# A decode block of attention and a ReLU layer: a weight piece split 126 to 2, a product in four column groups, and one head's softmax moved ahead of a loop

## The chip, the cores and the metric

The kernel runs on one core of a Trainium2 chip. The metric is device time in microseconds (us), lower is better. Before the change three runs gave 355.25, 355.38 and 355.55; the median is 355.38.

The core has five instruction streams that run side by side and wait for each other through semaphores: PE (TensorE, matrix products; its weight loads are listed as PEld), DVE (VectorE), ACT (ScalarE), POOL (GpSimd) and SP (SyncE, which here issues nearly all DMAs). Sixteen DMA engines move data between HBM and the on-chip memory SBUF. Matrix products land in PSUM.

## The reference

One token passes through a block whose layer norms are modulated by a condition `c`: grouped attention over a cache of 32768 positions (32 query heads, 8 key and value heads of 128), an output product, then a ReLU layer 512 to 1792 to 512.

```python
mod = (_silu(c) @ w_mod).reshape(c.shape[0], 6, 1, -1)     # sa, ca, ga, sb, cb, gb
h = _layernorm(x) * (1 + ca) + sa
q = (h @ wq) as 32 heads of 128
scores = q . k_cache / sqrt(128);  p = softmax(scores);  o = p . v_cache     # 4 query heads share one k, v
x = x + ga * (o @ wo)
h = _layernorm(x) * (1 + cb) + sb
x = x + gb * (relu(h @ w1) @ w2)
```

All inputs are bfloat16. The caches are 2 x 64 MB; with the weights 149 MB are read, and each byte is used once.

## The kernel before

**Data.** All bulk loads are issued by SP in one fixed order, the list `stream` (L139 to L144): w_mod, wq, K of head 0 in two pieces of 4 MB, then for each head the pieces of the next head's K and this head's V in turn, the last head's V in three pieces, wo in four pieces (WOP, L47: heads 0 to 3, 4 and 5, 6, 7), w1 in two, w2 in six (W2P, L51: 4, 3, 3, 2, 1 and 1 of 14 row blocks, 1 KB a row and block). `need(key)` (L147) issues the stream up to the piece that is asked for; `load` (L96) makes the destination. The destinations are five slots of a ring (L74), so an issue waits until the slot's last reader is done. An issue also waits for the eighth issue before it, because eight DMA semaphores take turns.

**A head.** K arrives as rows. `turn_k` (L405) transposes a quarter of a head's K on DVE in place (128x2048 words), `scores` (L422) multiplies each quarter with the queries (32 matmuls for half a head), and `bank_max` (L428) copies the half's scores to SBUF and takes maxima. `softmax` (L432 to L475) is a generator; each `next` does one step of it: m_p on DVE; the transpose mT on PE; Mrow and Mexp on DVE; the transpose Mb on PE, nbias and the exponentials P_g on ACT; their transpose PT_g and the sums Lexp on DVE; L_ps on PE; Linv on DVE. `pv` (L477) multiplies probabilities with V, 64 columns of steps in 32 matmuls for half a head. For heads 0 to 5, and the first half of head 6, these 32 stand in a hardware loop inside a section (L490 to L496) that is scheduled as one block; elsewhere they are written out. `blocks`, `o_cols` and `normalise` (L509 to L540) bring a head's output into a column and divide by the sums; `spread` (L544) and `project` (L555) multiply with wo.

**Order.** PE and DVE run in the order in which the program is written (L599). The main loop (L611) handles head g's V together with head g+1's K. In its second half it transposes and scores the second half of the next head's K, calls `bank_max`, starts the next head's softmax with one `next` (m_p), runs `pv(g, (2, 3))`, and does one more `next` (mT). The rest of that softmax is spread over the first half of the following round, between the four K quarters there (L618, L622, L631, L637, L640). With g = 6 the loop goes on differently (L653 to L664), then follow head 7's V, the wo product and the layer.

**The end.** Small filler products (`keep_clock`, L592) stand between the dependent steps. The attention output is brought into columns, `layernorm_T` (L250) makes the second layer norm, meanwhile `four_rows` (L331) turns the residual into four rows of 128 with a product whose weights are `rowpick`, 128x4. w1's product goes to four rows of PSUM at partitions 0, 32, 64 and 96 (L714), is transposed on DVE (L724), and ReLU on ACT (L725) writes it into `hid_bd`, which holds for each row block and each quarter i of the output a 128x4 matrix that is zero but for column i. The last product (L735) is 14 x 4 matmuls, each with such weights of four columns and 128 columns of w2, all adding into one 4x128 tile, `ffn_ps`. Two DVE products (L740, L742) apply gb and the residual, and SP stores four rows of 128.

Of the kernel before, what the change touches and what calls it, by code (L numbers as in the profile page):

```python
# [9 lines left out]
BF16 = mybir.dt.bfloat16  # L10
F32 = mybir.dt.float32
ACT = mybir.ActivationFunctionType
# [5 lines left out]
def kernel(  # L18
# [31 lines left out]
    LOOPED = Hkv - 2  # L50
    W2P = [(0, 4), (4, 7), (7, 10), (10, 12), (12, 13), (13, 14)]  # L51
    W1P = [(0, KT - 1), (KT - 1, KT)]
    assert Dh == 128 and REP == 4 and D == 512 and FT == W2P[-1][1] and NTILE == 4
    scale = float(Dh) ** -0.5
    eps = 1e-5
# [5 lines left out]
    vv = A_v_cache[0].rearrange("g (p j) d -> g p j d", p=P)  # L61
    wm_v = w_mod.rearrange("(p kt) n -> p kt n", p=P)
    wq_v = A_wq.rearrange("(p kt) n -> p kt n", p=P)
    def wo_v(i):
        g0, n = WOP[i]
        return A_wo[g0 * REP * Dh:(g0 + n) * REP * Dh, :].rearrange("(p r) d -> p r d", p=P)

    w1_v = B_w1.rearrange("(p kt) f -> p kt f", p=P)
    w2_v = B_w2.rearrange("(p f) d -> p f d", p=P)

# [19 lines left out]
    def piece(name, at, n):  # L90

        if name not in pieces:
            pieces[name] = ring.tile([P, 2 * TK * Dh], BF16, tag="slot", name=name)
        return pieces[name][:, at:at + n]

    def load(key):  # L96
        kind = key[0]
        if kind == "wm":
            t = ring.tile([P, KT, 6 * D], BF16, tag="slot", name="wm_sb")
            src = wm_v  # L100
        elif kind == "wq":
            t = ring.tile([P, KT, Hq * Dh], BF16, tag="slot", name="wq_sb")
            src = wq_v
        elif kind in "kv":
            g, steps = key[1], key[2]
            src = (kv if kind == "k" else vv)[g, :, TK * steps[0]:TK * (steps[-1] + 1), :]
            name = "Ksb" if kind == "k" else "Vsb"
            if len(steps) == 2:
                t = ring.tile([P, TK * len(steps), Dh], BF16, tag="slot", name=name)
            else:  # L110
                t = piece(name, TK * Dh * (steps[0] % 2), TK * Dh).rearrange("p (j d) -> p j d", d=Dh)
        elif kind == "wo":
            g0, n = WOP[key[1]]
            t = piece("wo_sb", g0 * REP * D, n * REP * D).rearrange("p (r d) -> p r d", d=D)
            src = wo_v(key[1])
        elif kind == "w1":
            k0, k1 = W1P[key[1]]
            t = piece("w12_sb", k0 * Dff, (k1 - k0) * Dff).rearrange("p (kt f) -> p kt f", f=Dff)
            src = w1_v[:, k0:k1]
        else:  # L120
            f0, f1 = W2P[key[1]]
            t = piece("w12_sb", KT * Dff + f0 * D, (f1 - f0) * D).rearrange("p (f d) -> p f d", d=D)
            src = w2_v[:, f0:f1]
        stream_dma(t[:], src)
        if kind in "kv":
            for i, u in enumerate(steps):
                loaded[(kind, g, u)] = t[:, TK * i:TK * (i + 1), :]
        else:
            loaded[key] = t[:]

    def stream_dma(dst, src):
        i = nc.sync.dma_start(out=dst, in_=src)
        tc.stamp_issue_order_token(i.ins, "sp_stream")
        if last_loop:

            tc.add_manual_dep(i.ins, last_loop[0], mybir.DependencyInfo(
                mybir.DependencyClass.NoSync, mybir.DependencyReason.DATA))

    stream = [("wm",), ("wq",)] + [("k", 0, (2 * G, 2 * G + 1)) for G in range(NG)]  # L139
    for g in range(LAST):  # L140
        for G in range(NG):
            stream += [(kind, gg, (2 * G, 2 * G + 1)) for kind, gg in (("k", g + 1), ("v", g))]
    stream += [("v", LAST, (0, 1)), ("v", LAST, (2,)), ("v", LAST, (3,))] + [("wo", i) for i in range(len(WOP))]
    stream += [("w1", i) for i in range(len(W1P))] + [("w2", i) for i in range(len(W2P))]  # L144
    pos = [0]

# [37 lines left out]
    for n in sorted({n * REP for _, n in WOP}):  # L184
# [21 lines left out]
    nc.vector.tensor_reduce(  # L206
        out=place32[:], in_=ident_f[:].rearrange("p (j m) -> p m j", m=32), op=ALU.add, axis=AX.X,
    )
    rowpick = const.tile([P, KT], F32)
    nc.vector.tensor_reduce(  # L210
        out=rowpick[:], in_=ident_f[:].rearrange("p (j m) -> p j m", m=32), op=ALU.add, axis=AX.X,
    )
    hid_bd = const.tile([P, FT, KT, KT], BF16)
    nc.gpsimd.memset(hid_bd[:], 0.0)

    pick8 = const.tile([16, 8], BF16)
    nc.vector.tensor_tensor(out=pick8[:], in0=ident_bf[0:16, 0:8], in1=ident_bf[0:16, 8:16], op=ALU.add)
# [22 lines left out]
    def bank(name):  # L240
        return ps_s.tile([P, 512], F32, tag="s", name=name)[:]
# [88 lines left out]

    def four_rows(e, name):  # L331

        r_ps = bank(f"{name}_ps")[0:KT, 0:P]
        nc.tensor.matmul(  # L334
            r_ps, lhsT=rowpick[:], rhs=e[:].rearrange("p m kt -> p (m kt)"), start=True, stop=True,
        )
        return r_ps

    gb_rows = const.tile([KT, P], F32)
    nc.scalar.copy(out=gb_rows[:], in_=four_rows(expand(modT_sb[:, 5 * KT:6 * KT], "gb"), "gb"))  # L340

    hT = const.tile([P, KT], BF16)
# [36 lines left out]
    def build_qbd(g):  # L379
        d_ap = qbd[g % 2][:]  # L380
        d_ps = d_ap.ap[0][0]
        s_ap = qrep_sb[:]
        s_ps = s_ap.ap[0][0]
        for a in range(4):
            o = AP(d_ap.tensor, d_ap.offset + (32 * a) * d_ps + 4 * 7 + 32 * a,
                   [[d_ps, 32], [QW, 4], [1, 4]])
            i = AP(s_ap.tensor, s_ap.offset + (32 * a) * s_ps + REP * g,
                   [[s_ps, 32], [Hq, 4], [1, 4]])
            nc.scalar.copy(out=o, in_=i)  # L389
# [209 lines left out]
    with tc.manual_schedule(engines={mybir.EngineType.PE, mybir.EngineType.DVE}):  # L599
# [10 lines left out]
        soft = None  # L610
        for g in range(LAST):  # L611
            h = g + 1
            build_qbd(h)
            turn_k(h, 0, 0)
            turn_k(h, 0, 1)
            turn_k(h, 1, 0)
            scores(h, 0, 0)
            if soft:  # L618
                next(soft)
            open_o(g)  # L620
            scores(h, 0, 1)
            if soft:  # L622
                next(soft)
            if g > 0:
                blocks(g - 1)
            scores(h, 1, 0)
            if g > 0:
                o_cols(g - 1)
            turn_k(h, 1, 1)
            scores(h, 1, 1)  # L630
            if soft:  # L631
                next(soft)
            if g > 0:
                normalise(g - 1)
                if g in [sum(w) for w in WOP]:
                    spread(part_of(g - 1))
            if soft:  # L637
                next(soft)
            bank_max(h, 0)
            next(soft or iter(()), None)  # L640
            pv(g, (0, 1))
            for u in (2, 3):
                for half in range(2):
                    turn_k(h, u, half)
                    scores(h, u, half)
            bank_max(h, 1)
            soft = softmax(h)
            next(soft)
            if g < LOOPED:
                pv(g, (2, 3))  # L650
                next(soft)
                continue
            next(soft)  # L653
            next(soft)
            pv(g, (2,), range(6))
            next(soft)
            next(soft)
            open_o(LAST)
            pv(g, (2,), range(6, 16))
            pv(g, (3,))  # L660
            next(soft)
            next(soft, None)
            a_rows.append(row_bank("a_ps"))
            blocks(g)  # L664
# [38 lines left out]

        keep_clock(3)
        layernorm_T(x1T[:], stat2, h2T[:], modT_sb[:, 3 * KT:4 * KT], ncb[:], "ln2", meanwhile)
        x1_rows = const.tile([KT, P], F32)
        nc.vector.tensor_copy(out=x1_rows[:], in_=x1_ps[0])

        NQ = 32 * FT
        for part, (k0, k1) in enumerate(W1P):  # L710
# [8 lines left out]
        keep_clock(3)  # L719
        hidT = rows_sb("hidT").rearrange("p a b -> p (a b)")[:, 0:NQ].rearrange("p (f e) -> p f e", e=32)  # L720
        hid_v = hid_ps[:, 0:NQ].rearrange("p (e f) -> p f e", f=FT)
        hb = hid_bd[:]
        for f0, f1 in ((0, FT // 2), (FT // 2, FT)):
            nc.vector.transpose(out=hidT[:, f0:f1], in_=hid_v[:, f0:f1])  # L724
            nc.scalar.activation(  # L725
                out=AP(hb.tensor, hb.offset + KT * KT * f0, [hb.ap[0], [KT * KT, f1 - f0], [KT + 1, KT]]),
                in_=hidT[:, f0:f1, 0:1].to_broadcast([P, f1 - f0, KT]), func=ACT.Relu,
            )

        ffn_ps = bank("ffn_ps")[0:KT, 0:P]  # L730
        for part, (f0, f1) in enumerate(W2P):
            w2_sb = need(("w2", part))
            for ft in range(f0, f1):
                for i in range(KT):
                    nc.tensor.matmul(  # L735
                        ffn_ps, lhsT=hid_bd[:, ft, i, :], rhs=w2_sb[:, ft - f0, i * P:(i + 1) * P],
                        start=(ft == 0 and i == 0), stop=(ft == FT - 1 and i == KT - 1),
                    )
        o_rows = const.tile([KT, P], F32)
        nc.vector.tensor_tensor(out=o_rows[:], in0=ffn_ps, in1=gb_rows[:], op=ALU.mult)  # L740
        o_bf = const.tile([KT, P], BF16)
        nc.vector.tensor_tensor(out=o_bf[:], in0=o_rows[:], in1=x1_rows[:], op=ALU.add)  # L742
    nc.sync.dma_start(out=out[0, 0].rearrange("(i n) -> i n", i=KT), in_=o_bf[:])


# [28 lines left out]
```

## Time and profile before

| | |
|---|---|
| median of three runs | 355.38 us (355.25 to 355.55) |
| the profiled execution: its time, and the span of its records | 355.74 us, 353.9 us |
| PE busy | 279.8 us (79%) |
| DVE busy | 203.1 us (57%) |
| ACT, POOL busy | 25.4 us, 3.9 us |
| HBM read | 149.42 MB, 422 GB/s over the span |
| last product's matmuls (L735) | 347.89 to 351.20 |

The span is the time from the first to the last record of one execution. Times below are counted from its start, so a line "307.78 7.12" is work that began at 307.78 us and took 7.12. A wait is named by what ended it. "Issue to landing" of a DMA is the time from its issue on SP to its last byte's semaphore. The granted clock is the share of TensorE's full clock that the hardware let through.

### The profile page before, as it was taken

What the parts mean: (1) busy time and instruction counts of PE and PEld (TensorE: products, weight loads), DVE (VectorE), ACT (ScalarE), POOL (GpSimd) and SP (SyncE); (2) the same over time, 40 slices, a digit from 0 to 9 for tenths busy, and PEclk for the clock granted to TensorE, in tenths of its full rate; (3) what the DMA queues carried; (4) which work ended last, traced back from release to release, by engine and by line L of the source; (5) the groups of instructions that cost most, each with busy time, mean ns of one, the idle gap of its engine ahead of it and who ended that gap; (6) DMA issues with size and microseconds to landing.
All of it is one profiled execution on the core that took longest, in us unless ns stands there. A gap on an engine that the chain in (4) does not pass through costs nothing. (4 is left out here: it accounts for less than half of the span.)

```text
span 353.9 us, 4006 instructions
## 1 busy us (share of the span) xinstructions
PE 279.8 (79%) x1311; PEld 112.7 (32%) x1311; DVE 203.1 (57%) x271; ACT 25.4 (7%) x69; POOL 3.9 (1%) x16
## 2 busy tenths in 40 slices
PE   0542781999898979897979796979689687989996
PEld 0221230333343323332323232323234233334444
DVE  6245775882768268462939178553938095734142
ACT  1220003000010001000100001000100010002000
POOL 4000000000000000000000000000000000000000
PEclk9995997799899999998999899999999997999999
DMA  8999999999999999999999999999999999999994
GB/s 309 455 422 445 431 422 441 441 418 424 459 418 422 459 418 424 441 437 426 433 444 417 430 456 419 427 446 426 422 448 430 422 439 441 422 430 424 421 420 177
DMA packets 6852, 149.59 MB, mean 423 GB/s; under 512 B 824, under 2 KB 1080, under 8 KB 1976
## 3 DMA queue, kind: packets, MB, share of 16 engines
q1 hardware_dynamic: 6776, 149.43, 98.4%
q8 instruction: 8, 0.13, 0.1%
q14 instruction: 4, 0.03, 0.0%
q0 software_dynamic: 64, 0.00, 0.0%
HBM read 149.42 MB, written 0.00 MB: 422 GB/s over the span
## 5 line engine op out<-in xcount | busy, mean ns | idle before, releaser
L405 DVE STREAM_TRANSPOSE Ksb<-Ksb 128x2048 f32<-128x2048 f32 x64 | 142.9, 2281 | 63.9 <-DMA Ksb<-in_A_k_cache_dram 63.9
L484 PE MATMUL o_ps<-Vsb,PT_g 128*16 (+1 forms) x512 | 130.0, 395 | 21.5 <-ACT qbd L389 7.2
L422 PE MATMUL S_ps<-Ksb,qbd 128*128 128x512 bf16 x512 | 121.8, 388 | 23.5 <-DVE Ksb L405 21.9
L422 PEld LDWEIGHTS <-qbd 128*128 128x128 bf16 x512 | 49.0, 98 | 87.6 <-issue 31.8
L484 PEld LDWEIGHTS o_ps<-Vsb,PT_g 128*16 x416 | 37.4, 90 | 90.2 <-issue 63.7
L428 DVE TENSOR_SCALAR_CACHE_REDUCE S_g<-S_ps 128x512 f32<-128x512 f32 x16 | 11.0, 690 | 34.4 <-PE S_ps L422 34.4
L389 ACT COPY qbd<-qrep_sb 32x16 bf16<-32x16 bf16 x32 | 6.4, 201 | 138.7 <-PE S_ps L422 137.6
L465 DVE STREAM_TRANSPOSE PT_g<-P_g 128x1024 bf16<-128x1024 bf16 x8 | 9.7, 1218 | 6.6 <-ACT P_g L459 6.6
L484 PEld LDWEIGHTS <-PT_g 128*16 128x16 bf16 x96 | 8.2, 90 | 11.0
L456 ACT ACTIVATE nbias<-Mb_ps 128x1 f32<-128x1 f32 x8 | 1.4, 171 | 136.8 <-PE Mb_ps L454 136.8
L459 ACT ACTIVATE P_g<-S_g,nbias 128x1024 bf16<-128x1024 f32 x8 | 9.2, 1148 | 0.2
L227 PE MATMUL xc_ps<-cx_sel,cx_bd 16*128 16x2 bf16 x4 | 0.3, 172 | 11.1 <-DVE cx_bd L221 11.1
L515 DVE SCALAR_TENSOR_TENSOR Y<-o_ps,smask,Y 16x128 f32<-16x128 f32 x24 | 8.1, 339 | 0.8
L471 PE MATMUL L_ps<-Lexp,ones_f 128*128 128x4 f32 x16 | 3.0, 257 | 4.3 <-DVE Lexp L468 4.3
L597 PE MATMUL spare_ps<-qbd,ident_bf 128*128 128x512 bf16 x19 | 5.6, 380 | 0.0
L440 PE MATMUL mT_ps<-ident_f,m_p 128*1 128x128 f32 x8 | 2.2, 270 | 3.9 <-DVE m_p L437 2.0
L471 PEld LDWEIGHTS L_ps<-Lexp,ones_f 128*128 128x128 f32 x16 | 3.1, 221 | 5.8 <-issue 5.1
L443 DVE TENSOR_REDUCE Mrow<-mT_ps 1x4 f32<-1x128 f32 x8 | 2.1, 257 | 4.6 <-PE mT_ps L440 4.6
L534 DVE TENSOR_TENSOR oT_sb<-acc_ps,Linv 128x4 bf16<-128x4 f32 x8 | 1.2, 150 | 5.7 <-PE acc_ps L521 5.7
L295 PE MATMUL mod_ps<-wm_sb,siluT 128*1 128x512 bf16 x24 | 3.6, 624 | 1.0 <-DVE siluT L289 1.0
L505 DVE MEMSET o_ps<- 16x512 f32 x8 | 3.9, 485 | 0.8
L552 DVE CAST o_sb<-o_ps 128x4 bf16<-128x4 f32 (+2 forms) x4 | 0.7, 167 | 5.7 <-PE o_ps L548 5.7
(115 smaller groups left out, 80.0 us busy)
## 6 DMA issues: line engine op xcount, KB each, us to landing
Ksb<-in_A_k_cache_dram SPq DMA_DIRECT2D x16, 4096.0 KB, 35.6
Vsb<-in_A_v_cache_dram SPq DMA_DIRECT2D x15, 4096.0 KB, 35.2
wq_sb<-in_A_wq_dram SPq DMA_DIRECT2D x1, 4096.0 KB, 19.6
Vsb<-in_A_v_cache_dram SPq DMA_DIRECT2D x2, 2048.0 KB, 31.8
wm_sb<-in_w_mod_dram SPq DMA_DIRECT2D x1, 3072.0 KB, 10.4
wo_sb<-in_A_wo_dram SPq DMA_DIRECT2D x1, 2048.0 KB, 29.1
w_sb<-in_B_w_dram SPq DMA_DIRECT2D x1, 1344.0 KB
wo_sb<-in_A_wo_dram SPq DMA_DIRECT2D x1, 1024.0 KB, 31.1
```

Of the source, the lines that this page charges most:

```text
L295: nc.tensor.matmul(dst[j // 4][32 * (j % 4):32 * (j % 4) + 1, :], lhsT=src_T[:, kt:kt + 1], rhs=w[:, kt, j * 512:(j + 1) * 512], start=(kt ...
L389: nc.scalar.copy(out=o, in_=i)
L405: t = nc.vector.transpose(out=KTt.bitcast(F32), in_=KTt.bitcast(F32))
L422: nc.tensor.matmul(S_ps_tiles[g], lhsT=qbd[g % 2][:, hp, 4 * (7 - s):4 * (7 - s) + P], rhs=KTv[:, 16 * sl:16 * sl + 16, h, :, par], start= ...
L428: nc.vector.tensor_scalar(out=S_tiles[g][:, G, :], in0=S_ps_tiles[g], scalar1=1.0, scalar2=None, op0=ALU.mult, op1=ALU.max, accum_out=m_ti ...
L459: nc.scalar.activation(out=P_g[:], in_=S_g[:].rearrange("p g f -> p (g f)"), func=ACT.Exp, bias=nbias[:], scale=scale, accum_out=l_g[:],)
L465: nc.vector.transpose(out=PT_g[:], in_=P_g[:])
L471: nc.tensor.matmul(L_ps[:], lhsT=ones_f[:], rhs=Lexp[:], start=True, stop=True)
L484: nc.tensor.matmul(o_tiles[g][:], lhsT=PT, rhs=Vx, start=False, stop=False, skip_group_check=True)
L505: nc.vector.memset(o_tiles[g][:], 0.0)
L515: nc.vector.scalar_tensor_tensor(out=Y[:], in0=o[:, s], scalar=smask[:, s:s + 1], in1=Y[:], op0=ALU.mult, op1=ALU.add,)
L597: nc.tensor.matmul(spare[0], lhsT=ident_bf[:], rhs=qbd[0][:, :, 0:P], start=True, stop=True)
```

## The change

1. The second piece of w2 (`EVEN`) is loaded by two DMAs, partitions 0 to 125 and 126 to 127, instead of one.
2. wo's last two pieces (heads 6 and 7) are loaded by one DMA instead of two.
3. `rowpick` is 128x128 with the four picking columns at 0, 32, 64 and 96, so that `four_rows` puts its rows on these partitions. gb's rows, the residual's rows and the output rows use all 128 partitions. The store takes every 32nd.
4. The hidden vector is kept plainly, 128x14 (`hid`). Each of the 56 matmuls of the last product has one column of it as weights and writes one row, at partition 32 i for quarter i, so four different column groups of the array are used in turn. `ffn_ps` is zeroed by DVE ahead of w1's product, and all matmuls add to it.
5. In the round g = 5, four more steps of head 6's softmax (mT; Mrow and Mexp; Mb, nbias and P_g; PT_g and Lexp) are written ahead of `pv(5, (2, 3))`; L_ps follows it.
6. In the round g = 6 (`ahead`), the fourth K quarter of the first half is transposed with the first three, Linv follows directly, and all four quarters are scored before `o_cols(5)`.

```diff
@@ -50,6 +50,7 @@
     LOOPED = Hkv - 2
     W2P = [(0, 4), (4, 7), (7, 10), (10, 12), (12, 13), (13, 14)]
     W1P = [(0, KT - 1), (KT - 1, KT)]
+    EVEN, EVEN_ROWS = ("w2", 1), 126
     assert Dh == 128 and REP == 4 and D == 512 and FT == W2P[-1][1] and NTILE == 4
     scale = float(Dh) ** -0.5
     eps = 1e-5
@@ -61,10 +62,6 @@
     vv = A_v_cache[0].rearrange("g (p j) d -> g p j d", p=P)
     wm_v = w_mod.rearrange("(p kt) n -> p kt n", p=P)
     wq_v = A_wq.rearrange("(p kt) n -> p kt n", p=P)
-    def wo_v(i):
-        g0, n = WOP[i]
-        return A_wo[g0 * REP * Dh:(g0 + n) * REP * Dh, :].rearrange("(p r) d -> p r d", p=P)
-
     w1_v = B_w1.rearrange("(p kt) f -> p kt f", p=P)
     w2_v = B_w2.rearrange("(p f) d -> p f d", p=P)
 
@@ -110,9 +107,10 @@
             else:
                 t = piece(name, TK * Dh * (steps[0] % 2), TK * Dh).rearrange("p (j d) -> p j d", d=Dh)
         elif kind == "wo":
-            g0, n = WOP[key[1]]
-            t = piece("wo_sb", g0 * REP * D, n * REP * D).rearrange("p (r d) -> p r d", d=D)
-            src = wo_v(key[1])
+            parts = key[1]
+            (g0, n), m = WOP[parts[0]], len(parts)
+            t = piece("wo_sb", g0 * REP * D, m * n * REP * D).rearrange("p (g x) -> p g x", g=m)
+            src = A_wo[g0 * REP * Dh:(g0 + m * n) * REP * Dh, :].rearrange("(g p r) d -> p g (r d)", g=m, p=P)
         elif kind == "w1":
             k0, k1 = W1P[key[1]]
             t = piece("w12_sb", k0 * Dff, (k1 - k0) * Dff).rearrange("p (kt f) -> p kt f", f=Dff)
@@ -121,10 +119,15 @@
             f0, f1 = W2P[key[1]]
             t = piece("w12_sb", KT * Dff + f0 * D, (f1 - f0) * D).rearrange("p (f d) -> p f d", d=D)
             src = w2_v[:, f0:f1]
-        stream_dma(t[:], src)
+        cuts = [0, EVEN_ROWS, P] if key == EVEN else [0, P]
+        for a, b in zip(cuts, cuts[1:]):
+            stream_dma(t[a:b], src[a:b])
         if kind in "kv":
             for i, u in enumerate(steps):
                 loaded[(kind, g, u)] = t[:, TK * i:TK * (i + 1), :]
+        elif kind == "wo":
+            for m, i in enumerate(parts):
+                loaded[("wo", i)] = t[:, m].rearrange("p (r d) -> p r d", d=D)
         else:
             loaded[key] = t[:]
 
@@ -140,7 +143,7 @@
     for g in range(LAST):
         for G in range(NG):
             stream += [(kind, gg, (2 * G, 2 * G + 1)) for kind, gg in (("k", g + 1), ("v", g))]
-    stream += [("v", LAST, (0, 1)), ("v", LAST, (2,)), ("v", LAST, (3,))] + [("wo", i) for i in range(len(WOP))]
+    stream += [("v", LAST, (0, 1)), ("v", LAST, (2,)), ("v", LAST, (3,))] + [("wo", parts) for parts in ((0,), (1,), (2, 3))]
     stream += [("w1", i) for i in range(len(W1P))] + [("w2", i) for i in range(len(W2P))]
     pos = [0]
 
@@ -206,12 +209,13 @@
     nc.vector.tensor_reduce(
         out=place32[:], in_=ident_f[:].rearrange("p (j m) -> p m j", m=32), op=ALU.add, axis=AX.X,
     )
-    rowpick = const.tile([P, KT], F32)
+    rowpick = const.tile([P, P], F32)
+    nc.gpsimd.memset(rowpick[:], 0.0)
     nc.vector.tensor_reduce(
-        out=rowpick[:], in_=ident_f[:].rearrange("p (j m) -> p j m", m=32), op=ALU.add, axis=AX.X,
+        out=rowpick[:].rearrange("p (j z) -> p j z", z=32)[:, :, 0],
+        in_=ident_f[:].rearrange("p (j m) -> p j m", m=32), op=ALU.add, axis=AX.X,
     )
-    hid_bd = const.tile([P, FT, KT, KT], BF16)
-    nc.gpsimd.memset(hid_bd[:], 0.0)
+    hid = const.tile([P, FT], BF16)
 
     pick8 = const.tile([16, 8], BF16)
     nc.vector.tensor_tensor(out=pick8[:], in0=ident_bf[0:16, 0:8], in1=ident_bf[0:16, 8:16], op=ALU.add)
@@ -330,13 +334,13 @@
 
     def four_rows(e, name):
 
-        r_ps = bank(f"{name}_ps")[0:KT, 0:P]
+        r_ps = bank(f"{name}_ps")[:, 0:P]
         nc.tensor.matmul(
             r_ps, lhsT=rowpick[:], rhs=e[:].rearrange("p m kt -> p (m kt)"), start=True, stop=True,
         )
         return r_ps
 
-    gb_rows = const.tile([KT, P], F32)
+    gb_rows = const.tile([P, P], F32)
     nc.scalar.copy(out=gb_rows[:], in_=four_rows(expand(modT_sb[:, 5 * KT:6 * KT], "gb"), "gb"))
 
     hT = const.tile([P, KT], BF16)
@@ -610,10 +614,15 @@
         soft = None
         for g in range(LAST):
             h = g + 1
+            ahead = h == LAST
             build_qbd(h)
             turn_k(h, 0, 0)
             turn_k(h, 0, 1)
             turn_k(h, 1, 0)
+            if ahead:
+                turn_k(h, 1, 1)
+                next(soft, None)
+                soft = None
             scores(h, 0, 0)
             if soft:
                 next(soft)
@@ -624,10 +633,13 @@
             if g > 0:
                 blocks(g - 1)
             scores(h, 1, 0)
+            if ahead:
+                scores(h, 1, 1)
             if g > 0:
                 o_cols(g - 1)
-            turn_k(h, 1, 1)
-            scores(h, 1, 1)
+            if not ahead:
+                turn_k(h, 1, 1)
+                scores(h, 1, 1)
             if soft:
                 next(soft)
             if g > 0:
@@ -646,6 +658,9 @@
             bank_max(h, 1)
             soft = softmax(h)
             next(soft)
+            if g == LOOPED - 1:
+                for _ in range(4):
+                    next(soft)
             if g < LOOPED:
                 pv(g, (2, 3))
                 next(soft)
@@ -703,8 +718,10 @@
 
         keep_clock(3)
         layernorm_T(x1T[:], stat2, h2T[:], modT_sb[:, 3 * KT:4 * KT], ncb[:], "ln2", meanwhile)
-        x1_rows = const.tile([KT, P], F32)
+        x1_rows = const.tile([P, P], F32)
         nc.vector.tensor_copy(out=x1_rows[:], in_=x1_ps[0])
+        ffn_ps = bank("ffn_ps")[:, 0:P]
+        nc.vector.memset(ffn_ps, 0.0)
 
         NQ = 32 * FT
         for part, (k0, k1) in enumerate(W1P):
@@ -719,28 +736,23 @@
         keep_clock(3)
         hidT = rows_sb("hidT").rearrange("p a b -> p (a b)")[:, 0:NQ].rearrange("p (f e) -> p f e", e=32)
         hid_v = hid_ps[:, 0:NQ].rearrange("p (e f) -> p f e", f=FT)
-        hb = hid_bd[:]
         for f0, f1 in ((0, FT // 2), (FT // 2, FT)):
             nc.vector.transpose(out=hidT[:, f0:f1], in_=hid_v[:, f0:f1])
-            nc.scalar.activation(
-                out=AP(hb.tensor, hb.offset + KT * KT * f0, [hb.ap[0], [KT * KT, f1 - f0], [KT + 1, KT]]),
-                in_=hidT[:, f0:f1, 0:1].to_broadcast([P, f1 - f0, KT]), func=ACT.Relu,
-            )
-
-        ffn_ps = bank("ffn_ps")[0:KT, 0:P]
+            nc.scalar.activation(out=hid[:, f0:f1], in_=hidT[:, f0:f1, 0], func=ACT.Relu)
+
         for part, (f0, f1) in enumerate(W2P):
             w2_sb = need(("w2", part))
             for ft in range(f0, f1):
                 for i in range(KT):
                     nc.tensor.matmul(
-                        ffn_ps, lhsT=hid_bd[:, ft, i, :], rhs=w2_sb[:, ft - f0, i * P:(i + 1) * P],
-                        start=(ft == 0 and i == 0), stop=(ft == FT - 1 and i == KT - 1),
+                        ffn_ps[32 * i:32 * i + 1, :], lhsT=hid[:, ft:ft + 1], rhs=w2_sb[:, ft - f0, i * P:(i + 1) * P],
+                        start=False, stop=(ft == FT - 1), skip_group_check=True,
                     )
-        o_rows = const.tile([KT, P], F32)
+        o_rows = const.tile([P, P], F32)
         nc.vector.tensor_tensor(out=o_rows[:], in0=ffn_ps, in1=gb_rows[:], op=ALU.mult)
-        o_bf = const.tile([KT, P], BF16)
+        o_bf = const.tile([P, P], BF16)
         nc.vector.tensor_tensor(out=o_bf[:], in0=o_rows[:], in1=x1_rows[:], op=ALU.add)
-    nc.sync.dma_start(out=out[0, 0].rearrange("(i n) -> i n", i=KT), in_=o_bf[:])
+    nc.sync.dma_start(out=out[0, 0].rearrange("(i n) -> i n", i=KT), in_=o_bf[::32, :])
 
 
 # ---- launch: one core; inputs and outputs as the reference has them ----
```

## The prediction

> **What bounds the kernel now.** I read the share of busy time first and put it aside: the page has the DMA engines at 9 tenths in 39 of 40 slices, at 422 GB/s, and PE at 79%, so neither is free. What ends last is asked of the chain of waits, in order of time (start, length, what):
>
> ```profile
> 307.78 7.12 PE S_ps L422 x32
> ...
> 341.80 0.51 PE acc_ps L567 x16
> ...
> 345.25 0.31 PE x_ps L334 x2
> ...
> 346.10 0.94 PE hid_ps L714 x16
> ...
> 347.89 3.30 PE ffn_ps L735 x56
> ...
> 351.22 0.29 DVE o_rows L740
> ```
>
> From 307.78 to 351.20 it is TensorE nearly without a break, and the last product alone takes 3.30 us of it. The reader should ask how far behind the data is. The stretches of the end answer (length, busy time of PE, PEld, DVE, ACT, POOL, granted clock, DMA share, GB/s):
>
> ```profile
> 348.00:348.50 0.50, 0.50 (x11) 0.50 (x10) 0.00 (x0) 0.08 (x1) 0.00 (x0) 1.00 0.82 307
> 348.50:349.00 0.50, 0.50 (x13) 0.50 (x10) 0.00 (x0) 0.00 (x0) 0.00 (x0) 1.00 0.66 242
> 349.00:349.65 0.65, 0.65 (x16) 0.65 (x13) 0.00 (x0) 0.00 (x0) 0.00 (x0) 1.00 0.45 158
> 349.65:350.25 0.60, 0.60 (x15) 0.60 (x13) 0.00 (x0) 0.00 (x0) 0.00 (x0) 1.00 0.06 22
> ```
>
> Sixteen times the share is the number of engines at work: 13, 11, 7, and then 0.06 x 16 = 1. One engine of sixteen works alone for 0.6 us, and the last piece of w2 (issued at 341.81, 8.7 to landing) is there at 350.5. The last four matmuls start near 350.95. So TensorE is only 0.4 us behind the data: a faster product is worth little more than that unless the data ends sooner. For the softmax I read the timeline around head 5's last V loop:
>
> ```profile
> 275.09 0.69 DVE L428 TENSOR_SCALAR_CACHE_REDUCE S_g<-S_ps 128x512 f32<-128x512 f32 x1 [1.99 <-PE S_ps L422]
> 275.71 0.08 DVE L428 DVE_READ_ACCUMULATOR S_g<-S_ps 128x1 f32 x1
> 275.82 0.15 DVE L437 TENSOR_REDUCE m_p<-m 128x1 f32<-128x2 f32 x1
> 276.84 0.57 PEld L484 LDWEIGHTS o_ps<-Vsb,PT_g 128*16 x4 [2.29 <-issue]
> ```
>
> and the stretches behind it:
>
> ```profile
> 276.80:286.30 9.50, 8.19 (x32) 2.72 (x32) 2.79 (x2) 0.00 (x0) 0.00 (x0) 1.00 1.01 438
> 286.30:298.60 12.30, 9.33 (x39) 4.27 (x39) 10.58 (x18) 1.41 (x3) 0.00 (x0) 0.88 0.99 428
> 298.60:307.60 9.00, 8.94 (x32) 3.27 (x32) 4.61 (x3) 0.00 (x0) 0.00 (x0) 0.78 0.98 422
> ```
>
> The loop starts 0.87 us after m_p, which it does not read: the waits list puts that 1.8 us to "DVE m_p". A looped section waits for everything traced ahead of it on DVE. And 12.3 us between two loops hold 9.3 of TensorE: DVE's softmax rows stand between the K turns.
>
> **The softmax moved.** Now four more steps precede the loop: mT and Mb on PE, Mrow, Mexp, PT_g and Lexp on DVE, nbias and P_g on ACT. Head 0's softmax, which nothing interrupts, prices them: maxima done 53.83, Lexp done 59.39, less a table load of 1.28, is 4.28. So Lexp ends at 275.79 + 4.25 = 280.05, and the loop starts 0.85 later, near 280.9: 4.0 late. The array idles from 275.05. Half clock follows such gaps: in 292.2 to 295.6 PE was busy 1.67 of 3.40, and 295.6 to 302.5 was granted 0.51. In this loop that has cost little: the one from 161.28 ran 9.01 us at clock 0.81, those from 238.19 and 276.8 took 8.71 and 9.4 at 1.00, because the loop's own control sets its rate. I take 9.4, ends 8.7 and 9.8. It ends at 290.3, not 286.3.
>
> Behind it L_ps 0.3, then 32 score matmuls without a gap (7.11, as at 307.78): the four K turns begin at 283.51 with the landing and take 8.9, to 292.4, so each is done in time. Scores end near 298.2. Then, all after them: o_cols 0.3, two products of normalise 0.5, spread and its copy 0.45, bank_max 0.75, section start 0.14 to 0.8. The next loop starts at about 300.4, against 298.65. It runs 8.03, the length at full clock (259.48 to 267.5), not 8.94. TensorE is then **0.85 us late** at the scores of the last K pieces (landing 302.9, turned by 311.9, not limiting); ends -0.1 and +2.3, the latter with the 0.9 of half clock again. So this part costs rather than gains. SP's queue: the V piece issued at 286.45 goes out 4 us later, but landed only at 322.2, 35 us after issue, with three 4 MB pieces ahead of it; no DMA runs dry.
>
> [...]
>
> **wo's last two pieces as one DMA.** Same bytes, one issue fewer, w2's split one issue more. They landed at 340.5 and 341.8 (issue 308.61 + 31.9, 309.08 + 32.7). project(2), at 341.42 now, has to wait for 341.8: nothing if TensorE is 0.85 late, 0.4 if it is not late at all. The DMA lanes shift by one: a piece waits for the eighth before it, so the last w2 piece waits for w1's first (landing near 345.1) instead of wo's last (341.8). It then has some 3 us of queued bytes ahead of it; out's store needs 0.8 from issue to packets. Free.
>
> **rowpick 4 to 128 columns.** The weight load of x_ps grows from 0.08 to the 0.15 to 0.19 of a 128-column float32 load, twice: 0.1 on the path (0 to 0.2). The same at the front lies under wq's landing. memset of rowpick on POOL replaces that of hid_bd (0.30) and DVE has 2.3 us of waiting for cx_row there. ffn_ps's memset (0.12 to 0.48 by the 128x512 row of 0.48) lies in DVE's gap from 346.2 to 347.07; at worst it is still covered. Relu writes 128x7 instead of 128x28: 0.0 to 0.05. Tail copies and products keep 128 elements a partition, 0.28 each; out still has four rows of 256 B.
>
> **The last product.** L735's matmuls start every 55.8 ns: (350.96 - 347.89) / 55. In four column groups the nearest row is hid_ps: 16 matmuls of 448 columns in 0.94, when one alone is shown as 350 ns, so four share a pass. With 128 columns a pass of four takes at best one old matmul, 56 ns, and at worst a weight load, 85 ns: 13 passes are 0.73 to 1.1, and the last matmul's 0.22 on top: 0.95 to 1.3 instead of 3.30. I take 1.1, for passes bound by streaming as in hid_ps. TensorE alone would now end at 347.89 + 0.85 + 0.1 + 1.1 = **349.9**. That is before the data: the new bound is the last landing, plus 0.13 (wq: landing to matmul), 0.01, 0.22.
>
> **126 and 2 rows.** 126 rows of 3 KB do not divide over sixteen engines; over fourteen it is nine each, and two engines get none. A row of 3 KB is 0.12 us at 422/16 = 26 GB/s. If the engine that works alone is one of the two, it ends 8 x 0.12 = 0.95 sooner and the others, which end at 349.65, 0.12 to 0.24 later: the landing moves from 350.5 to 350.1 or 350.2. If it is not, it is 0.12 to 0.24 later, 350.65. No row names the engine. I take the first, because one lagging engine is what the last 0.6 us consists of, and keep both ends. [...]
>
> **Sum** against the profiled execution (355.74 around a span of 353.94; the median of the runs is 355.38, 0.36 lower, and I carry the difference over). Product ends now: 351.20. After: 350.15 + 0.36 = 350.5. Gain 0.7, that is 354.7. Changes under 0.2%, 0.71 us, are about what a measurement cannot tell from none.
>
> **Rivals.**
> 1. *The lone engine keeps its rows.* Landing 350.65, end 351.0: 355.2. For it: nothing names the engine. Against: only that two are relieved.
> [...]
> 3. *The column groups do not overlap at 128 columns.* 3.30 stays: 347.89 + 0.95 + 3.30 = 352.1: 356.3. Against: hid_ps.
>
> **How the numbers follow.** Forecast 0.52 (354.7, own range 354.4 to 354.95: landing 350.0 to 350.2, TensorE late by up to 1.6), rival 1 0.30, rival 2 0.12, rival 3 0.04, others 0.02. The forecast straddles the bound of 354.67: two thirds of it count as faster, 0.35; the rest with rival 1 as same, 0.48; rivals 2 and 3 and half the others as slower, 0.17. The range goes from 354.35 to 355.7, leaving out rivals 2 and 3 and a little below.
>
> **What would show it.** Right: the loop of head 5 starts near 280.9 and the next near 300.4; PE waits for DMA w_sb inside L735; the last landing at 350.1; no stretch with a share of 0.06. Wrong: a granted clock of 0.5 reaching past 288, ffn_ps starting after 350, or a lone engine still at work at 350.3.

## The result, and the profile after

The changed kernel takes **357.1 us** (median of six runs, 356.87 to 357.44) against 355.25 us (355.06 to 355.55) for the kernel before in the same comparison: ratio 1.005, 95% interval 1.004 to 1.006. That is 1.85 us or 0.5% slower. The forecast was 354.7 us, with a range up to 355.7, which does not hold it.

The profiled execution took 356.87 us around a span of 355.1; the one of before had 355.74 around 353.9. The two profiles are therefore only 1.13 us apart: before's profile lies 0.4 us above its median, after's 0.2 below. What differs between them has to be read with that in mind.

The chain of waits of the changed kernel, in order of time (start, length, what), its end:

```profile
313.60 31.15 DMA w_sb<-in_B_w_dram
...
344.76 6.76 DMA w_sb<-in_B_w_dram
...
351.56 0.26 PE ffn_ps L747 x4
```

Before, the last 43 us were TensorE's. Now they are the data's: the first of the two DMA rows is w1's first piece, which lands at 344.74. The last piece of w2 is the eighth issue after it, so it is issued then, at 344.76, and lands at 351.52; only the last four matmuls follow. The issue is 3 us later than before (341.81), but that is not what moves the landing: in a run below the same piece is issued at 345.01 and lands at 350.50. The bound is where the prediction put it, but the last landing is at 351.52 instead of the 350.15 that the sum used, and instead of 350.5 before.

The timeline of the changed kernel for the last product and the store (start, length, engine, line, operation; in brackets the idle time before it and what ended that):

```profile
348.87 0.86 PE L747 MATMUL ffn_ps<-w_sb,hid 128*1 128x128 bf16 x28
350.30 0.34 PE L747 MATMUL ffn_ps<-w_sb,hid 128*1 128x128 bf16 x12 [0.57 <-DMA w_sb<-in_B_w_dram]
350.94 0.84 PE L747 MATMUL ffn_ps<-w_sb,hid 128*1 128x128 bf16 x16 [0.30 <-DMA w_sb<-in_B_w_dram]
...
352.48 0.62 SPq L755 DMA_DIRECT2D out_dram<-o_bf  x1
```

The 56 matmuls are indeed cheap: 28 in 0.86, 12 in 0.34, against 3.30 for all before. But they stop twice for w2, and the store's issue at the end takes 0.62 where it took 0.35. The data's side stands in the stretches (length, then busy time of PE, PEld, DVE, ACT, POOL with numbers of instructions, granted clock, DMA share, GB/s). Before:

```profile
345.50:347.00 1.50, 1.50 (x20) 0.46 (x20) 0.57 (x3) 0.08 (x1) 0.00 (x0) 1.00 1.02 398
347.00:348.00 1.00, 0.88 (x9) 0.26 (x6) 0.71 (x2) 0.42 (x2) 0.00 (x0) 1.00 1.04 404
348.00:349.00 1.00, 1.00 (x20) 1.00 (x19) 0.00 (x0) 0.08 (x1) 0.00 (x0) 1.00 0.74 275
```

and after:

```profile
345.50:347.00 1.50, 1.50 (x5) 0.52 (x4) 0.85 (x5) 0.20 (x1) 0.00 (x0) 0.50 1.00 252
347.00:348.00 1.00, 1.00 (x17) 0.31 (x16) 0.00 (x0) 0.00 (x0) 0.00 (x0) 0.81 1.03 239
348.00:349.00 1.00, 0.98 (x19) 0.34 (x19) 0.71 (x2) 0.32 (x2) 0.00 (x0) 1.00 1.05 235
```

All sixteen engines are at work (share 1.00 to 1.05), and they move 252 and 239 GB/s where they moved 398 and 404. Busy engines that move less: each packet takes longer. The trace's packet records say how much (median of the packets that began in the half microsecond from the time named):

| from | before, 3 KB | before, 4 KB | after, 3 KB | after, 4 KB |
|---|---|---|---|---|
| 345.0 | 121 ns | 159 ns | 121 ns | 159 ns |
| 346.0 | 121 | 159 | 195 | 266 |
| 347.0 | 121 | - | 202 | 280 |
| 348.0 | 121 | - | 227 | - |

The 4 KB packets are those of w2's first piece, which nobody changed, and some of the 3 KB packets those of its third. (The 280 is a single packet.) So the second piece, cut at row 126, slows its neighbours too while it is in flight, from about 345.3 to 349. The granted clock of 0.50 in the first stretch is a second difference; which of the two costs the time is the first thing to tell apart.

### The profile page after: what moved, and what is told of

It is laid out like the page before. It is cut to its first block, busy times and chain, and to the rows that moved or that the text cites. A ratio compares the mean times of both kernels' runs of the same rounds, so it can differ in the third digit from the quotient of the medians.

```text
span 355.1 us, 4008 instructions
## 1 busy us (share of the span) xinstructions
PE 280.8 (79%) x1311; PEld 111.6 (31%) x1311; DVE 203.5 (57%) x272; ACT 25.4 (7%) x69; POOL 3.9 (1%) x16
## 5 line engine op out<-in xcount | busy, mean ns | idle before, releaser
L601 PE MATMUL spare_ps<-qbd,ident_bf 128*128 128x512 bf16 x19 | 6.7, 446 | 0.0
L366 PE MATMUL q_ps<-wq_sb,hT 128*1 128x512 bf16 x32 | 3.6, 627 | 1.7 <-DMA wq_sb<-in_A_wq_dram 1.7
```

Of the source, the lines that this page charges most:

```text
L366: nc.tensor.matmul(q_ps[i][32 * a:32 * a + 1, :].rearrange("o (h e) -> o h e", e=32), lhsT=hT[:, kt:kt + 1], rhs=wq_f[:, kt, i, a], start= ...
L601: nc.tensor.matmul(spare[0], lhsT=ident_bf[:], rhs=qbd[0][:, :, 0:P], start=True, stop=True)
```

## Experiments

The theory from these rows was that **the shape of the cut piece** slows the transfers: 126 rows instead of 128. Its rivals: **the clock** (the wait for the merged wo brings on half clock, and the product comes late); **the count** (one DMA more in the queue, whatever its shape); **the engines** (fourteen instead of sixteen carry the piece, by the landings counted below). Beside these stood the store from every 32nd partition, and whether any part of the change gains. Ratios are against the kernel before in the same comparison, with 95% intervals.

### The piece of w2

**Undo the split alone**, in the changed kernel:

```diff
-        cuts = [0, EVEN_ROWS, P] if key == EVEN else [0, P]
+        cuts = [0, P]
```

> The changed kernel with w2's second piece loaded by one DMA of 128 rows again; all else as changed. Split theory (the 126-row DMA slows all DMA engines: 3 KB packets from 345.5 to 349 took about 200 ns instead of 121): the rate between 345.5 and 349 comes back from 240 to 390 GB/s, the last landing goes from 351.5 to about 350.5, and the time from 357.1 to 356.1 to 356.4. Clock theory (the loss is the half clock after the wait for the merged wo piece): DMA rate unchanged, 357.1 stays. Store theory (strided store): 357.1 stays.

Measured: 355.66 us, against 355.31 for before, ratio 1.001 (1.0002 to 1.0019); that is 1.44 less than the changed kernel, and 0.4 below the range that the split theory gave. The stretches are before's again:

```profile
345.50:347.00 1.50, 1.31 (x19) 0.40 (x18) 0.77 (x5) 0.00 (x0) 0.00 (x0) 1.00 0.99 386
347.00:348.00 1.00, 0.98 (x19) 0.35 (x18) 0.70 (x2) 0.43 (x2) 0.00 (x0) 1.00 1.04 405
```

The last landing is at 350.25, the product ends at 350.55.

**The split alone**, in the kernel before:

```diff
-        stream_dma(t[:], src)
+        cuts = [0, 126, P] if key == ("w2", 1) else [0, P]
+        for a, b in zip(cuts, cuts[1:]):
+            stream_dma(t[a:b], src[a:b])
```

> The kernel before with nothing changed but w2's second piece split into 126 and 2 rows. Split theory: last landing 1.0 later, at 351.5, product's end at 351.9 instead of 351.2, time 355.9 to 356.3. Clock and store theories: 355.25 as before. My prediction on record: 0.2 to 0.7 faster or 0 to 0.1 slower.

Measured: 357.03 against 355.31, ratio 1.0057 (1.0043 to 1.007). Its stretches:

```profile
345.50:347.00 1.50, 1.24 (x11) 0.30 (x6) 0.70 (x2) 0.19 (x1) 0.00 (x0) 1.00 1.07 281
347.00:348.00 1.00, 0.00 (x1) 0.00 (x1) 0.02 (x1) 0.31 (x2) 0.00 (x0) 1.00 1.01 254
```

The rate is down at a granted clock of 1.00, with the old product and the old wo. From both sides one line carries the loss. The last landing is at 351.51, 1.0 later than before. The 1.72 us are 0.7 more than the split theory's range allowed; some 0.35 of them is time after the store has landed (last section), which leaves about 1.4, as from the other side.

**wo in four pieces again**, in the changed kernel:

```diff
-    stream += [("v", LAST, (0, 1)), ("v", LAST, (2,)), ("v", LAST, (3,))] + [("wo", parts) for parts in ((0,), (1,), (2, 3))]
+    stream += [("v", LAST, (0, 1)), ("v", LAST, (2,)), ("v", LAST, (3,))] + [("wo", parts) for parts in ((0,), (1,), (2,), (3,))]
```

> The changed kernel with wo's last two pieces as two DMAs again. Clock theory: project(2) starts near 340.5 instead of 341.52, no half clock at 344 to 347.4, the last product starts near 347.3 instead of 348.87, and the time falls by 0.6 to 1.0 to 356.1 to 356.5. Split theory: the product still waits for the last landing at 351.5, 356.9 to 357.1.

Measured: 357.31, ratio 1.0057 (1.0044 to 1.007), no gain. There project(2) starts at 340.13 instead of 341.52 and `hid_ps` at 344.79 instead of 347.01, so TensorE is two microseconds earlier, and the product waits for w2 all the same (timeline of this kernel):

```profile
348.02 0.39 PE L747 MATMUL ffn_ps<-w_sb,hid 128*1 128x128 bf16 x16 [1.24 <-DMA w_sb<-in_B_w_dram]
```

The theory of the clock falls: without half clock (1.00 in 344 to 347.4) the time is no shorter, and 0.2 above the split theory's range. This kernel has one DMA more than the changed one, and with it the longer tail of the last section.

**Other cuts by rows**, each in the kernel before, with 64, 120 or 112 in place of 126 in the edit above. At 120, the 15 landings (below) make eight rows an engine, as in the whole piece, where 16 landings stand for 128 rows.

> The kernel before with w2's second piece split into 64 and 64 rows: sixteen engines carry both parts. [...] Engine-count theory (what hurts is that 14 engines instead of 16 carry the piece): rate stays near 390, 355.3.

> [...] Rows-an-engine theory (nine rows where eight fit is what disturbs): rate near 390, 355.3.

> [...]

| cut | us | before | ratio (95%) | GB/s |
|---|---|---|---|---|
| 126 + 2 | 357.03 | 355.31 | 1.0057 (1.0043 to 1.007) | 261 in 345.5 to 349 |
| 64 + 64 | 357.31 | 355.37 | 1.0053 (1.0039 to 1.0067) | 271 |
| 120 + 8 | 357.12 | 355.40 | 1.0045 (1.0029 to 1.006) | 269 |
| 112 + 16 | 357.11 | 355.40 | 1.0043 (1.0028 to 1.0059) | 252 |
| none (before's profile) | | | | 364 |

The price is the same for all of them, within their intervals. Taken as one for each engine that carries a part, the landings in the traces give the number of engines: 16 for a whole piece, 14 and 2 for the cut 126 + 2 (in the changed kernel's trace each of these two parts shows one landing more, 0.5 and 0.4 us after its issue), 16 and 16 for 64 + 64, 15 and 8 for 120 + 8, 16 and 16 for 112 + 16. The rate does not follow that number: 261 GB/s with 14 and 2, 271 with 16 and 16. So the theory of the engines falls as the cause of the loss, and by the 269 GB/s of the cut at 120, with eight rows an engine, the theory of the rows an engine falls too.

**The same three blocks in two DMAs of 128 rows**, in the kernel before:

```diff
-        stream_dma(t[:], src)
+        if key == ("w2", 1):
+            stream_dma(t[:, 0:2], src[:, 0:2])
+            stream_dma(t[:, 2:3], src[:, 2:3])
+        else:
+            stream_dma(t[:], src)
```

> The kernel before with w2's second piece as two DMAs of all 128 rows, two row blocks and one (2 KB and 1 KB a row). Shape theory (fewer than 128 rows a DMA is what slows the engines): rate near 390 between 345.5 and 349, 355.3. Count theory (one DMA more in the last eight, whatever its shape, is what costs): 356.8 to 357.2, like the four row splits.

Measured: 355.89 against 355.34, ratio 1.0015 (1.0006 to 1.0024). Its stretch, and that of the 64 + 64 cut below it:

```profile
345.50:349.00 3.50, 3.35 (x47) 2.18 (x48) 0.83 (x3) 0.50 (x2) 0.00 (x0) 1.00 0.97 367
```

```profile
345.50:349.00 3.50, 2.03 (x29) 0.92 (x18) 0.71 (x2) 0.50 (x2) 0.00 (x0) 1.00 1.05 271
```

One DMA more, in 128 rows each, runs at before's rate, and the last landing is at 350.50, though the last piece is issued at 345.01. The count is not what slows the data. It has a smaller price of its own, which the shape theory's 355.3 left out: some 0.35 us of this kernel's 0.55 is time after the store has landed (last section).

**A larger piece cut**: the first of wo, 2 MB, in the kernel before, by the edit of the split alone with `("wo", 0)` for `("w2", 1)`.

> The kernel before with wo's first piece (2 MB) split into 126 and 2 rows, w2 whole. Rate theory (the engines move 126 rows at about 245 instead of 420 GB/s): 2.1 MB take 8.6 instead of 5.0 us, time 355.3 + 3.6 = 358.9 (357.9 to 359.5). Fixed-price theory (each such split costs about 1.7, whatever its size): 357.0. No effect ahead of the end: 355.3.

Measured: 362.86 against 355.40, ratio 1.0211 (1.0196 to 1.0227): 7.5 us. Its stretches:

```profile
332.00:334.00 2.00, 2.00 (x11) 0.82 (x10) 0.00 (x0) 0.00 (x0) 0.00 (x0) 1.00 1.07 242
334.00:336.00 2.00, 2.00 (x11) 0.73 (x9) 0.65 (x2) 0.00 (x0) 0.00 (x0) 1.00 0.85 188
...
338.00:340.00 2.00, 0.12 (x1) 0.00 (x0) 1.35 (x4) 0.00 (x0) 0.00 (x0) 1.00 1.19 216
340.00:342.00 2.00, 0.00 (x0) 0.00 (x0) 0.00 (x0) 0.00 (x0) 0.00 (x0) 1.00 0.79 158
```

Before moved 467, 381, 432 and 445 GB/s in these. So the larger piece has the larger price, and it is twice what the rate theory gave (7.5 against 3.6 us): the low rate lasted from 330 to 342, over the neighbours too. Here two of the sixteen engines finished the next piece at 335.55 and 338.38, the other fourteen between 343.56 and 345.24, and the 126 rows have 14 landings: two engines had no part of them. They ran ahead, and that did not help.

### The softmax, and the column groups

**Items 5 and 6 alone**, in the kernel before: the four steps of the softmax ahead of `pv`, and the `ahead` branches, as in the diff of the change.

> The kernel before with the softmax order alone (head 6's steps ahead of head 5's last V loop, and the four K quarters of head 7 scored in one go). My step on record (the section waits for Lexp, TensorE 0.85 late): the loop starts at 280.9, the scores of head 7 end at 315.7, time 356.0 or slower. Theory after the result (the section waits only for what PE has already seen, Mexp): the loop starts at 278.3, scores end near 313.6 instead of 314.9, TensorE 1.3 early up to w1's product, which then waits for its last piece at 346.0, and the last landing plus 0.4 caps the gain: 354.9 to 355.1.

Measured: 355.35 against 355.37, ratio 1.0 (0.9991 to 1.0009). No difference, and the time of neither theory.

**Items 3 and 4 alone**: the changed kernel without items 1, 2, 5 and 6.

```diff
-        cuts = [0, EVEN_ROWS, P] if key == EVEN else [0, P]
+        cuts = [0, P]
...
-    stream += [("v", LAST, (0, 1)), ("v", LAST, (2,)), ("v", LAST, (3,))] + [("wo", parts) for parts in ((0,), (1,), (2, 3))]
+    stream += [("v", LAST, (0, 1)), ("v", LAST, (2,)), ("v", LAST, (3,))] + [("wo", parts) for parts in ((0,), (1,), (2,), (3,))]
...
-            if g == LOOPED - 1:
-                for _ in range(4):
-                    next(soft)
...
-            ahead = h == LAST
+            ahead = False
```

> The kernel before with the four column groups, rows on partitions 0 to 96 and the strided store; no split, wo in four DMAs, softmax order as before. The last product shrinks from 3.30 to about 1.0 us of TensorE, but ends at the last landing plus 0.3, that is 0.3 to 0.6 earlier. Store theory (the store from every 32nd partition takes 0.5 longer): 355.2 to 355.5, no gain. If the store cost nothing: 354.7 to 355.0.

Measured: 355.74 against 355.37, ratio 1.0008 (0.9999 to 1.0017).

**Items 3 to 6**: the same edit without its last two hunks.

> The changed kernel without the split and with wo in four DMAs: softmax order and column groups together. Both only bring TensorE ahead of the data, so they do not add up: product's end at the last landing plus 0.3, store 0.5 longer: 355.2 to 355.5, as with the column groups alone. If wo's merging had cost time in the run without the split (355.66): 0.2 to 0.4 less than that run.

Measured: 355.78 against 355.37, ratio 1.0008 (0.9999 to 1.0017). The softmax gains nothing on top of the column groups, and the column groups gain nothing over the kernel before; both runs lie some 0.25 above the range that the store theory gave. The end of this kernel's timeline says why the second is so:

```profile
349.61 0.91 PE L747 MATMUL ffn_ps<-w_sb,hid 128*1 128x128 bf16 x16 [0.26 <-DMA w_sb<-in_B_w_dram]
...
351.21 0.65 SPq L755 DMA_DIRECT2D out_dram<-o_bf  x1
```

The product ends at 350.5, with the data, as it should. Then the store takes 0.65 to issue and lands at 352.86, 1.65 after its issue began. In the kernel before the issue is 0.35, from 351.84, and the landing at 353.02, 1.18. The run with w2 whole differs from this one in wo's pieces alone and took 355.66, so merging them cost nothing.

### The store

**Store partitions 0 to 3** instead of every 32nd, first in the changed kernel, then in the kernel with items 3 to 6:

```diff
-    nc.sync.dma_start(out=out[0, 0].rearrange("(i n) -> i n", i=KT), in_=o_bf[::32, :])
+    nc.sync.dma_start(out=out[0, 0].rearrange("(i n) -> i n", i=KT), in_=o_bf[0:4, :])
```

> The changed kernel with the final store taken from partitions 0 to 3 instead of 0, 32, 64 and 96. It leaves out three of the four output quarters (rows 1 to 3 hold zeros times gb plus nothing of them), the work is otherwise the same. Store theory: issue on SP 0.35 instead of 0.62 us, issue to landing 1.2 instead of 1.66, time 356.6. Split and clock theories: 357.1.

> The run with softmax order and column groups (no split, wo in four DMAs) with the store taken from partitions 0 to 3: it leaves out three of the four output quarters, the work is otherwise the same. Store theory: issue 0.3 instead of 0.65, issue to landing 1.15 instead of 1.65, time 0.5 less than that run: 355.2. If the store is not the price that hides the shorter product: 355.7.

Measured: 356.80 against 355.31, ratio 1.0039 (1.0026 to 1.0052), for the first; 355.10 against 355.34, ratio 0.9994 (0.9985 to 1.0003), for the second. In the second the issue and landing are before's (351.36 to 352.53, 1.17):

```profile
351.36 0.35 SPq L755 DMA_DIRECT2D out_dram<-o_bf  x1
```

Against 355.78 with the strided store the difference is 0.68; the traces show 0.48 of it, as the longer way from issue to landing (1.65 against 1.17). In the changed kernel it came out as 0.3 (356.80 against the 357.10 of another comparison), with intervals that overlap; there the data landed at 352.20 in the profiled execution, later than in the changed kernel's own. The gain that is left for the column groups with a cheap store is 0.24 and can't be told from none.

**Four stores of one row**, two issued by SP and two by ACT, in the kernel with items 3 to 6:

```diff
-    nc.sync.dma_start(out=out[0, 0].rearrange("(i n) -> i n", i=KT), in_=o_bf[::32, :])
+    rows = out[0, 0].rearrange("(i n) -> i n", i=KT)
+    for i in range(KT):
+        (nc.sync if i < 2 else nc.scalar).dma_start(out=rows[i:i + 1], in_=o_bf[32 * i:32 * i + 1, :])
```

> The run with softmax order and column groups (no split, wo in four DMAs), with the store of every 32nd partition replaced by four stores of one row, two on SP and two on ACT. Store theory: issue 0.3 each, two in a row 0.3 longer than one, against 0.55 for the strided one: 0.2 to 0.3 less than that run, 355.4 to 355.6, about the kernel before. If the strided store cost nothing: 0.3 more, 356.1.

Measured: 355.94 against 355.40, ratio 1.0014 (1.0005 to 1.0024). Issued from 351.17, landed at 352.80, 1.63: no gain. Each of the four lands 1.06 to 1.26 after its own issue began, about as fast as one store from neighbouring partitions; but the last is issued at 351.74, 0.57 after the first. So here it is the issues one after the other that cost the time, and not the partitions. In the strided store 0.3 of the 0.48 is the longer issue.

**The product turned round**, in the kernel with items 5 and 6: blocks of w2 are the weights, one column of `hid` moves, the output is 128 x 4 and is stored as 128 rows of 8 bytes.

```diff
-                        ffn_ps, lhsT=hid_bd[:, ft, i, :], rhs=w2_sb[:, ft - f0, i * P:(i + 1) * P],
+                        ffn_ps[:, ko:ko + 1],
+                        lhsT=w2_sb[:, ft - f0, :].rearrange("p (m ko) -> p ko m", ko=KT)[:, ko, :],
+                        rhs=hid[:, ft:ft + 1], start=False, stop=(ft == FT - 1), skip_group_check=True,
...
-    nc.sync.dma_start(out=out[0, 0].rearrange("(i n) -> i n", i=KT), in_=o_bf[:])
+    nc.sync.dma_start(out=out[0, 0].rearrange("(p kt) -> p kt", p=P), in_=o_bf[:])
```

> A version meant to beat both kernels: kernel before with the softmax order, and the last product turned round: w2's blocks are the weights and the hidden vector's column is streamed, as in project(3), so that the output stands as 128x4 columns, without rows of the residual and of gb. Product 56 pairs of 0.033 (project's rows), ends 0.4 after the last landing, DVE's two steps 0.16 instead of 0.28 each, and out is stored as 128 rows of 8 bytes. If that store costs what four rows cost (1.2 to landing): 354.7 to 355.0. If 128 small rows cost 0.5 more: 355.3.

Measured: 356.62 against 355.34, ratio 1.0038 (1.0024 to 1.0051). The product ends at 350.38 and the two DVE products take 0.16 each instead of 0.28, so the store is issued at 350.80, a microsecond sooner than in the kernel before. It lands at 353.65, 2.85 later, so the run is 1.3 above the highest time that was expected.

## Why the prediction was wrong

**The step that failed is "126 and 2 rows".** It was worked out as rows shared over engines, each packet at an unchanged 0.12 us, with ends of 0.4 sooner and 0.15 later for the landing. The runs show that the packets do not keep their length: 0.12 becomes 0.2, for the neighbours also. Landing 1.0 later, time 1.44 more (the changed kernel less the one without the split). The price of a row was read from full 128-row pieces, and no row of the trace showed a DMA into fewer partitions. The nearest rows were no bound for it, and a line such as "an unknown shape may run at a lower rate" had no place among the rivals; rival 1 kept the same packets and failed with the step. That fourteen engines carry the 126 rows came out as assumed (14 landings); that the lone engine was one of the two left out was not shown.

The choice of the better end also rested on an accident. One engine worked alone for 0.56 us at the end of before's profiled execution. The lag of the last engine behind the second to last was 0.07 in the run with w2 whole, 0.52 with the column groups alone, 0.19 with the softmax alone, 0.21 with both, 0.00 with the product turned round and 0.01 in the changed kernel: it differs from execution to execution. It may also be what put before's profile 0.4 us above its median, and so why the landing moved by 1.0 from profile to profile where the medians moved by more; that is not shown, and the column groups alone speak against it, whose profile has a lag of 0.52 and lies at its median (355.77, 355.74).

Why fewer rows slow the packets is not shown: no run watched what holds a packet up. The runs show what goes with it: in 345.5 to 349 the four cuts by rows moved 252 to 271 GB/s, whatever the number of engines, and the cut by blocks, with 128 rows in both DMAs, 367, against 364 for the whole piece.

**"Out still has four rows of 256 B"** failed as well: the bytes are the same, the partitions are not. 0.68 us, by the pair with and without the stride. No term of the sum stood for it.

**The softmax's step failed in its mechanism, and its worth came out right by luck,** because the data hides it. I had the section wait for Lexp on DVE, the loop start at 280.9, the next at 300.4, and the scores end 0.85 late. The timeline of the changed kernel:

```profile
276.48 0.22 DVE L452 COPY Mexp<-Mrow 1x128 f32<-1x128 f32 x1
276.75 0.22 PE L458 MATMUL Mb_ps<-ident_f,Mexp 1*128 1x1 f32 x1 [0.62 <-DVE Mexp L452]
...
278.25 0.59 PE L488 MATMUL o_ps<-Vsb,PT_g 128*16 x2 [1.29 <-issue]
278.48 1.25 DVE L469 STREAM_TRANSPOSE PT_g<-P_g 128x1024 bf16<-128x1024 bf16 x1 [1.79 <-ACT P_g L463]
```

The loop starts at 278.25, ahead of PT_g. So it does not wait for all the DVE work that is traced ahead of it. It comes behind what stands ahead of it on PE, which is Mb, and Mb needs Mexp; another 1.29 us passed before it started, for which the trace names no wait. What I had read from "the loop starts 0.87 after m_p" was one instance too few. The next loop began at 297.80 and the scores ended at 313.58, 1.3 earlier than in before's profile, not 0.85 later. That is no gain of the softmax: with the column groups alone, and the old order, the next loop began at 297.71 and the scores ended at 313.77. And it is hidden behind the data either way: 355.35 against 355.37. Half clock did come, 0.50 from 279.11 to 282.52, and the loop was no longer for it: 9.28 us, from 278.25 to 287.53, where 9.4 had been reckoned from before's loop at a clock of 1.00.

**wo's merged pieces**: right in the wait, not in its size and its company, and "Free" held, for the later issue of the last piece of w2 too. project(2) waited 1.05 us for the landing, not 0.4 or nothing, because TensorE was early and not late:

```profile
341.52 0.70 PE L571 MATMUL acc_ps<-o_sb,wo_sb 128*128 128x1 bf16 x16 [1.05 <-DMA wo_sb<-in_A_wo_dram]
```

In this execution half clock followed from 344 to 347.4, and `hid_ps` began at 347.01 instead of 346.09. With wo in four pieces the product waited for w2 all the same, so it cost nothing.

**The last product** was right: the 16 matmuls that stand together take 0.39, 28 take 0.65 at full clock; four share a pass of 56 ns ((0.39 - 0.22) / 3 = 0.057) as forecast; 3.30 goes, TensorE is done before the data, and the product ends 0.30 after the last landing (351.52 to 351.82) where 0.36 was reckoned. Rival 3 did not come. Its worth was forecast as 0.7 with the landing moved; with the landing where it was, 0.24 is left. The **x_ps** term was right too: at full clock (w2 whole) its two weight loads take 0.40 in place of 0.09, and `x_ps` 0.38 as before. One reading was off without harm: the page before shows 38, not 39, of 40 slices at 9 tenths.

The sum as it should have stood: split 1.44, store 0.68, product and softmax -0.24: 1.88, where 1.85 was measured. These terms are the steps of one chain of runs from the changed kernel back to the one before, so that they add up proves nothing; they say how the loss is shared out. The profile named the next bound rightly, the landing of the data, and the loss came from the two edits that touch the data's way and that had been put at a gain and at nothing.

## What to carry to other kernels

Where a transfer ends the kernel, keep bulk loads at 128 partitions: cut a piece by blocks, not by rows. The piece cut by blocks here, with its neighbours, moved 367 GB/s, the pieces cut by rows 252 to 271 in place of 364, and around the cut piece of 2 MB 158 to 242 in place of 381 to 467. An edit that moves results to other partitions changes the store too; price the store's shape, from issue to landing, before counting what the compute saves. And a feature of one profiled execution, such as one engine that ends late, is a reason for an edit only when a second execution shows it again.

## What the runs showed that I had not expected

- A load of 384 KB cut at any of four rows cost 1.7 to 1.9 us (with the longer tail below), one of 2 MB 7.5 us.
- A store of the same 1 KB takes 1.17 us from issue to landing from four neighbouring partitions, 1.65 from four that are 32 apart, and 2.85 as 128 rows of 8 bytes.
- Kernels with more DMAs than before (the cuts in the kernel before, wo in four pieces beside the split, the blocks, the four stores) need about 1.3 us from the store's landing to the end of the span; the others 0.9 to 1.0. For the blocks it is 352.76 to 354.0, for the kernel before 353.02 to 353.9. The cause is open.
- Half clock from 344 to 347.4 in the changed kernel's profile followed a stretch in which PE was busy for most of the time. The stretches, which show it:

```profile
341.00:344.00 3.00, 2.48 (x46) 1.73 (x46) 0.26 (x3) 0.00 (x0) 0.00 (x0) 0.99 0.99 416
344.00:347.40 3.40, 3.40 (x18) 1.58 (x20) 1.88 (x13) 0.29 (x1) 0.00 (x0) 0.50 1.04 325
```

  PE was busy 2.48 of 3.00 us there, mostly with matmuls of one column; with w2 whole it was busy 2.80 of the same 3.00, and the clock stayed at 1.00. In the traces of the kernel before and of the changed one, every stretch of one clock lasts 3.41 us or a multiple of it, up to 92.16 (the last of a trace aside). From 30 us on the clock falls from full to half 6 times in the first and 8 times in the second. In the 3.41 us ahead of the fall PE was busy 13 to 49% of the time in 13 of these 14, and 71% ahead of this one. Why it fell here is not shown.
